# Mixing's state held by pairs of heads: four 64-column state products per batch instead of eight 32-column ones

## The chip, the cores and the metric

The kernel runs on one core of a Trainium2 chip. The metric is device time in microseconds (us) of one execution; lower is better. The time before is 571.9 us, the median of three runs (571.48 to 572.41).

## The reference, cut to what matters

The program is a chunked state-space mixer ("attention" in the names), followed by two MLPs over 3072 tokens with model width 256 and hidden width 2048. For 4 batches, 8 heads, 768 tokens, head width D = 32 and state width N = 16:

```python
for c in range(nc):                        # chunks of tokens
    cum = np.cumsum(log_a, axis=-1)        # log decay inside the chunk
    L = exp(cum[i] - cum[j]) * (i >= j)
    M = (C @ B.T) * L
    y_intra = M @ x                        # inside the chunk
    y_inter = (C @ state) * exp(cum)[:, None]   # from the chunks before
    y = y_intra + y_inter
    state = exp(cum[-1]) * state + (B * exp(cum[-1] - cum)).T @ x
h = softplus(y_all @ w_in) @ w_out         # first MLP
out = (lambda u: u * sigmoid(1.702 * u))(h @ w2_in) @ w2_out
```

Each head has a state of its own, 16 x 32 numbers.

## The kernel before, in words

**Units.** The mixer uses chunks of T = 128 tokens: NC = 6 chunks of NB = 4 batches, 24 sub-blocks s = 4 * chunk + batch, each with 8 heads. The first MLP takes one chunk of all batches (512 tokens) at a time and runs 96 steps t, 16 per chunk, each making one 128-row block of the hidden layer (`g1`) and, two steps later, adding its part of the output (`g2`). While step t works on chunk c, the mixer prepares sub-blocks of chunk c + 1, one sub-block per four steps (k = 0 to 3 is the step inside these four). The second MLP follows after step 95; it uses the `p` products and no mixing.

**Order.** All instructions are issued in the order written (`tc.manual_schedule`), so each engine works its own queue in program order. What the kernel's text does not say, semaphores do: a tile's reader waits for its writer, and a new tile in a pool's slot waits for those who used the slot's tile before. Before step 0 stands a start in which the four sub-blocks of chunk 0 are mixed one after another with the first weights being unpacked beside them (the names `wraw`, `wt`, `w1ih`, `w1il` belong to the unpacking of the 64-bit weights into a high and a low float part).

**Mixing of one sub-block.** `at_load_a` loads the decays: `abz` (for the mask L) and, from chunk 1 on, `ad`, the decays broadcast over 32 partitions per head, by four DMAs on SyncE's queue. `at_scan` makes L on VectorE. `at_small` makes `bs` (B times the decay to the chunk's end) on GpSimd, then the running decay `dc` by two scans on VectorE, and `cd` = C * dc on GpSimd. `at_cb` and `at_m` make M, written over L. `at_y` and `at_u` run for a pair of sub-blocks (s - 1, s with s odd) at k = 2: the state products (`y<-cd,st`), the products with M (`y<-L,px`) and the products that make the state's increment u (`y<-px,bs`). `at_out` copies y into the MLP's input `xh`, `xl`; `at_state` updates the state on VectorE.

**Layout of the state.** A head has a row group of 32 partitions, of which 16 hold the state and the other 16 are zero; heads 0 to 3 lie in the four row groups at g = 0, heads 4 to 7 in the same row groups at g = 1. For odd s the row groups are turned by one (`rows`), so that the eight products of one g of a pair use eight different 32 x 32 pieces of TensorE's array: 16 state products for a pair, each 32 partitions deep, 32 columns of weights wide, 128 columns long.

**PSUM.** Pool `ps_y` has two one-bank tiles, tag y, from the start to the end: sub-blocks use them for y and u, and in the last chunk and in the second MLP the output sums with an odd number (`acc_of`) take them, one bank for each half j of the output. Pool `ps_e` holds six banks until step 0.

**The end of the start.** `at_u(NB - 1)` (the increment of sub-block 3) comes after step 0's `g1`; `at_state(2)` and `at_state(3)` come in steps 1 and 3.

The functions touched by the diff follow with the line numbers of the profile.

Of the kernel before, what the change touches and what calls it, by code (L numbers as in the profile page):

```python
# [34 lines left out]
SX_X, SX_BN, SX_CI, SX_W = 0, 256, 384, 640  # L35
# [8 lines left out]
def mixer_two_mlps(ctx: ExitStack, tc: tile.TileContext, pack_p, pack_q, pack_s, pack_x, a_rows, consts, w1i, w1o, w2i, w2o, out):  # L44
# [20 lines left out]
    cc = at1.tile([P, 2 + P], F32, name="cc")  # L65
    zr = at1.tile([P, T], F32, name="zr")
    mB, mC, eye = cc[:, 0:1], cc[:, 1:2], cc[:, 2:]
# [5 lines left out]
    bs_t = [at1.tile([P, NH, 2, N], F32, name=f"bs{i}") for i in range(2)]  # L73
    state = [at1.tile([P, 2, D], F32, name=f"st{b}") for b in range(NB)]
# [102 lines left out]
    def rows(s, h):  # L177
        r = 32 * ((h + s % 2) % 4)
        return slice(r, r + 32)

# [4 lines left out]
    def at_load_a(s):  # L185
        c, b = divmod(s, NB)
        d = sub.setdefault(s, {})
        d["abz"] = at.tile([P, NH, T], F32, tag="abz", name=f"abz{s}")
        r0 = s * NH
        nc.sync.dma_start(  # L190
            out=d["abz"].rearrange("p h t -> p (h t)"),
            in_=scr_z[r0 : r0 + NH, :].rearrange("(o h) t -> o (h t)", o=1).to_broadcast([P, NH * T]),
        )
        if c > 0:
            d["ad"] = at.tile([P, 2, T], F32, tag="ad", name=f"ad{s}")
            src = scr_a[r0 : r0 + NH, :].rearrange("(g h) t -> h g t", g=2)
            for h in range(4):
                nc.sync.dma_start(out=d["ad"][rows(s, h)], in_=src[h : h + 1].to_broadcast([32, 2, T]))
# [43 lines left out]
    def at_spread(s, half):  # L242
        d = sub.setdefault(s, {})
        if s == 0:
            d["abz", half] = ps_y.tile([P, NH // 2, T], F32, tag="y", name=f"abz{s}_{half}")
# [21 lines left out]
    def at_small(s):  # L267
        c, b = divmod(s, NB)
        d = sub[s]
        if c < NC - 1:  # L270
            (nc.vector if s == 3 else nc.gpsimd).tensor_tensor(
                out=bs_t[s % 2][:, :, 0, :], in0=d["bn"].rearrange("p (h n) -> p h n", h=NH),
                in1=d["L"][:, :, T - 1 : T].to_broadcast([P, NH, N]), op=ALU.mult,
            )
        if c > 0:
            d["dc"] = at.tile([P, 2, T], F32, tag="dc", name=f"dc{s}")
# [4 lines left out]
            d["cd"] = at.tile([P, 2, T], F32, tag="cd", name=f"cd{s}")  # L281
            nc.gpsimd.tensor_tensor(
                out=d["cd"].rearrange("p g t -> p (g t)"), in0=d["dc"].rearrange("p g t -> p (g t)"), in1=d["ci"], op=ALU.mult
            )
# [44 lines left out]
    def y_of(s):  # L329
        if "y" not in sub[s]:  # L330
            sub[s]["y"] = ps_y.tile([P, 512], F32, tag="y", name=f"y{s}")
        return sub[s]["y"]

    def busy(s, n):
        for _ in range(n):
            nc.tensor.matmul(y_of(s)[:, 512 - P :], wz, wz, start=True, stop=True, skip_group_check=True)

    def at_y(*ss):
        for s in ss:
            y_of(s)  # L340


        for g in range(2 if ss[0] >= NB else 0):
            for h in range(4):
                for s in ss:
                    d, r = sub[s], rows(s, h)
                    nc.tensor.matmul(  # L347
                        d["y"][32 * h : 32 * h + 32, g * T : g * T + T], state[s % NB][r, g, :], d["cd"][r, g, :],
                        start=(g == 0), stop=False, skip_group_check=True,
                    )  # L350
        for s in ss:
            d = sub[s]
            for g in range(2):
                for h in range(4):
                    x0 = g * P + h * D
                    nc.tensor.matmul(  # L356
                        d["y"][32 * h : 32 * h + 32, g * T : g * T + T], d["x"][:, x0 : x0 + D], d["M", g][:, h, :],
# [3 lines left out]
    def at_u(s):  # L361
        d = sub[s]
        if s < NSUB - NB:
            for g in range(2):
                for h in range(4):
                    x0 = g * P + h * D
                    nc.tensor.matmul(
                        d["y"][rows(s, h), 256 + g * D : 256 + g * D + D],
                        bs_t[s % 2][:, 4 * g + h].rearrange("p s n -> p (s n)"), d["x"][:, x0 : x0 + D],
                        start=True, stop=True, skip_group_check=True,  # L370
                    )
# [3 lines left out]
    def at_out(s):  # L375
# [6 lines left out]
        y = d["y"][:, 0:256].rearrange("p (g t) -> p g t", g=2)  # L382
# [7 lines left out]
    def at_state(s):  # L390
# [4 lines left out]
        u = d["y"][:, 256 : 256 + 2 * D].rearrange("p (g d) -> p g d", g=2)  # L395
        st = state[b]
        if c == 0:
            if s < 2:
                nc.scalar.activation(st, u, AF.Copy)
            else:  # L400
                nc.vector.tensor_copy(st, u)
            return
        for g in range(2):
# [72 lines left out]
    with tc.manual_schedule():  # L476
# [8 lines left out]
        idle = ps_y.tile([P, 512], F32, tag="y", name="idle")  # L485
# [30 lines left out]
        for i in range(2):  # L516
            nc.gpsimd.memset(bs_t[i][:, :, 1, :], 0.0)
# [90 lines left out]
        w_load(w1i, "1i", 3)  # L608
        early_ctx.close()
# [412 lines left out]
```

## Time and profile before

| what | value |
|---|---|
| median of three runs | 571.9 us |
| the profiled execution | 572.09 us |
| its span in the trace | 570.3 us |
| TensorE busy | 562.7 us, 99% of the span |
| VectorE busy | 452.7 us, 79% |
| ScalarE busy | 338.9 us, 59% |
| GpSimd busy | 122.0 us, 21% |

The profiled execution is 1.8 us longer than its span, which covers the instructions of the engines alone. Busy time is a union: products that run at the same time in different pieces of the array count once. In the trace a float32 product has two records (it passes the array twice); an fp32r product has one. PE stands for TensorE's products, PEld for its weight loads, DVE for VectorE, ACT for ScalarE, POOL for GpSimd and SPq for SyncE's DMA queue.

### The profile page before, as it was taken

Reading aid. Unit: us, or ns where it says so; the run is one execution under the profiler, and the core shown is the slowest. Engines: PE = TensorE matmul, PEld = TensorE weight load, DVE = VectorE, ACT = ScalarE, POOL = GpSimd, SP = SyncE. Lnnn points to the kernel's source line nnn. Section 1 sums busy time; section 2 is a strip of 40 time slices with the busy share of each in tenths; the row PEclk is TensorE's granted clock in tenths of the full one; section 3 lists DMA queues with packets and bytes.
Section 4 is the critical chain, followed back from the end, with each engine's and each line's share of the span. In section 5 each row is a group of like instructions: output and inputs, shape, how many; then the busy total and the mean of one; then the engine's idle time right before and its main releaser. Section 6 shows DMA issues by size and latency. Waiting matters only on the chain.

```text
span 570.3 us, 9042 instructions
## 1 busy us (share of the span) xinstructions
PE 562.7 (99%) x3424; PEld 452.0 (79%) x3424; DVE 452.7 (79%) x683; ACT 338.9 (59%) x571; POOL 122.0 (21%) x105
## 2 busy tenths in 40 slices
PE   9999999999999999999999999999999999999997
PEld 7656687888888888888888788888888888888885
DVE  7997999979787977878898699998976565665654
ACT  4877654534344443435898877866756464664654
POOL 3343474444463544442000000000000000000000
PEclk9999999999999999999999999999999999999999
DMA  8766543343414335410323212000200000100002
GB/s 296 252 227 231 207 167 107 107 150 106 156 62 166 107 111 201 164 62 2 110 77 109 72 38 75 1 1 0 75 0 1 1 0 1 74 1 0 2 0 75
DMA packets 26427, 51.28 MB, mean 90 GB/s; under 512 B 3056, under 2 KB 8848, under 8 KB 26384
## 3 DMA queue, kind: packets, MB, share of 16 engines
q1 hardware_dynamic: 26240, 50.64, 26.1%
q8 instruction: 27, 0.44, 0.3%
q14 instruction: 16, 0.13, 0.1%
q10 hardware_dynamic: 144, 0.07, 0.0%
HBM read 47.35 MB, written 3.34 MB: 89 GB/s over the span
## 4 chain that ended last, share of the span: by engine, by line
PE 84%; DVE 5%; ACT 3%; DMA 3%; issue 1%; SPq 0%; POOL 0%; DVEq 0%; ACTq 0%
PE p L811 19%; PE h L427 19%; PE o L787 8%; PE o L785 8%; PE o L786 8%; PE o L446 6%; PE o L448 6%; PE o L447 6%; PE y L356 2%; DMA wraw_1i<-w1i 2%; PE cb L316 1%; PE y L347 1%; DVE L L262 1%; DVE L L326 1%; DVE gl L85 1%; DMA ad<-scr_a 1%
## 5 line engine op out<-in xcount | busy, mean ns | idle before, releaser
L85 DVE TENSOR_TENSOR gl<-g,gh 128x512 fp32r<-128x512 f32 x180 | 141.8, 789 | 22.7 <-ACT gh L453 21.7
L896 ACT ACTIVATE g<-h 128x512 f32<-128x512 f32 x96 | 57.6, 600 | 107.4 <-PE h L427 97.1
L453 ACT ACTIVATE gh<-g 128x512 fp32r<-128x512 f32 x180 | 113.8, 632 | 5.8
L427 PE MATMUL h<-xh,w1ih 128*128 128x512 f32 x192 | 79.4, 414 | 0.3 <-ACT w1ih L95 0.3
L427 PE MATMUL h<-xl,w1ih 128*128 128x512 f32 x192 | 75.3, 393 | 0.2 <-DVE xl L85 0.2
L817 DVE TENSOR_TENSOR g<-p,x 128x512 f32<-128x512 f32 x72 | 49.6, 689 | 29.6 <-PE p L811 28.1
L446 PE MATMUL o<-gh,w1ol 128*128 128x512 f32 x168 | 66.4, 395 | 0.3 <-DVE w1ol L85 0.3
L447 PE MATMUL o<-gh,w1oh 128*128 128x512 f32 x168 | 65.5, 390 | 0.0
L448 PE MATMUL o<-gl,w1oh 128*128 128x512 f32 x168 | 65.4, 389 | 0.0
L262 DVE TENSOR_TENSOR_SCAN L<-abz,eye 128x1024 f32<-128x1024 f32 (+1 forms) x25 | 64.3, 2580 | 0.8 <-PE abz L252 0.7
L427 PE MATMUL h<-xh,w1il 128*128 128x512 f32 x192 | 59.4, 391 | 0.8 <-DVE w1il L85 0.8
L819 ACT ACTIVATE g<-g 128x512 f32<-128x512 f32 x72 | 45.4, 631 | 20.9 <-DVE g L817 18.5
L88 POOL TENSOR_TENSOR rhs_bd<-tc,pk 64x512 fp32r<-64x512 f32 x32 | 54.9, 1714 | 1.2
L785 PE MATMUL o<-gh,w2ol 128*128 128x512 f32 x120 | 46.8, 390 | 0.4 <-ACT gh L453 0.4
L787 PE MATMUL o<-gl,w2oh 128*128 128x512 f32 x120 | 46.8, 390 | 0.0
L786 PE MATMUL o<-gh,w2oh 128*128 128x512 f32 x120 | 46.7, 389 | 0.0
L819 ACT ACTIVATE g<-p 128x512 f32<-128x512 f32 x24 | 14.3, 596 | 52.4 <-PE p L811 52.3
L427 PEld LDWEIGHTS h<-xh,w1ih 128*128 128x128 f32 x192 | 36.0, 188 | 9.8 <-issue 2.2
L427 PEld LDWEIGHTS h<-xh,w1il 128*128 128x128 f32 x192 | 36.0, 188 | 9.2 <-DVE w1il L85 1.2
L427 PEld LDWEIGHTS h<-xl,w1ih 128*128 128x128 f32 x192 | 36.0, 188 | 9.0 <-issue 2.4
L326 DVE TENSOR_TENSOR L<-cb,L 128x512 f32<-128x512 f32 x40 | 26.9, 682 | 15.9 <-PE cb L316 15.2
L446 PEld LDWEIGHTS o<-gh,w1ol 128*128 128x128 f32 x168 | 31.5, 188 | 7.7 <-DVE w1ol L85 0.7
(183 smaller groups left out, 1058.9 us busy)
## 6 DMA issues: line engine op xcount, KB each, us to landing
abz<-scr_z SPq DMA_DIRECT2D x20, 512.0 KB, 3.8
pk<-pack_s SPq DMA_DIRECT2D x16, 512.0 KB, 4.3
px<-pack_x SPq DMA_DIRECT2D x20, 320.0 KB, 3.0
wraw_1i<-w1i SPq DMA_DIRECT2D x8, 512.0 KB, 4.9
wraw_1o<-w1o SPq DMA_DIRECT2D x8, 512.0 KB, 4.5
wraw_2i<-w2i SPq DMA_DIRECT2D x8, 512.0 KB, 3.5
wraw_2o<-w2o SPq DMA_DIRECT2D x8, 512.0 KB, 3.3
out<-ot SPq DMA_DIRECT2D x11, 256.0 KB, 2.0
```

Source lines behind the costliest of these rows:

```text
L85: nc.vector.tensor_sub(o, x, y)
L262: nc.vector.tensor_tensor_scan(out=d["L"][:, h].rearrange("p h t -> p (h t)"), data0=ab.rearrange("p h t -> p (h t)"), data1=eye8[:, h].re ...
L427: nc.tensor.matmul(h, w[:, k, f], x[:, k, :], start=(n == 0), stop=(n == 5))
L446: nc.tensor.matmul(a, w1ol[:, m, o], d["gh"], start=first, stop=False)
L447: nc.tensor.matmul(a, w1oh[:, m, o], d["gh"], start=False, stop=False)
L448: nc.tensor.matmul(a, w1oh[:, m, o], d["gl"], start=False, stop=last)
L453: nc.scalar.activation(d["gh"], d["g"], AF.Copy)
L785: nc.tensor.matmul(a, wl, d["gh"], start=first, stop=False)
L786: nc.tensor.matmul(a, wh, d["gh"], start=False, stop=False)
L787: nc.tensor.matmul(a, wh, d["gl"], start=False, stop=last)
L811: nc.tensor.matmul(dst, w, x, start=start and i == 0, stop=i == 2, skip_group_check=not start)
L819: nc.scalar.activation(d["g"], src, AF.Gelu_apprx_sigmoid)
```

## The change

Two neighbouring heads share a row group of 32 partitions, 16 for each, so that the eight heads of a sub-block fill the 128 partitions once. The state tile is [128, 64]: for each head's 16 rows it holds the 32 columns of both heads of the pair, and a mask (`own`, 1 in the head's own columns) gives `state_own`, a masked copy made on GpSimd by `at_state`. A state product is then 32 partitions deep and 64 columns of weights wide, four for a sub-block. The increments u are made by pairs as well: four products with 64 columns. `bs` has no zero half any more; `ad` is one DMA of [128, 128]; `dc` is one scan, `cd` is 128 columns wide, the state update is one instruction. Both sub-blocks of a pair share one tile of two banks in `ps_y` (bank g for heads 4g to 4g + 3). In the start the tiles of y come from `ps_a`, which is released with `ps_e`; so `at_u(3)`, `at_state(2)` and `at_state(3)` are moved ahead of step 0. The odd output sums take `ps_y`'s two banks as one tile.

```diff
-SX_X, SX_BN, SX_CI, SX_W = 0, 256, 384, 640
+SX_X, SX_BN, SX_CI, SX_W = 0, 256, 384, 512
...
-    ps_y = ps_ctx.enter_context(tc.tile_pool(name="ps_y", bufs=2, space=PSUM))
-
     early_ctx = ExitStack()
+    ps_a = early_ctx.enter_context(tc.tile_pool(name="ps_a", bufs=2, space=PSUM))
     ps_e = early_ctx.enter_context(tc.tile_pool(name="ps_e", bufs=1, space=PSUM))
...
-    cc = at1.tile([P, 2 + P], F32, name="cc")
+    cc = at1.tile([P, 2 + P + 2 * D], F32, name="cc")
...
-    bs_t = [at1.tile([P, NH, 2, N], F32, name=f"bs{i}") for i in range(2)]
-    state = [at1.tile([P, 2, D], F32, name=f"st{b}") for b in range(NB)]
+    bs_t = [at1.tile([P, NH, N], F32, name=f"bs{i}") for i in range(2)]
+    state = [at1.tile([P, 2 * D], F32, name=f"st{b}") for b in range(NB)]
+    state_own = [at1.tile([P, 2 * D], F32, name=f"so{b}") for b in range(NB)]
...
-            d["ad"] = at.tile([P, 2, T], F32, tag="ad", name=f"ad{s}")
-            src = scr_a[r0 : r0 + NH, :].rearrange("(g h) t -> h g t", g=2)
-            for h in range(4):
-                nc.sync.dma_start(out=d["ad"][rows(s, h)], in_=src[h : h + 1].to_broadcast([32, 2, T]))
+            d["ad"] = at.tile([P, T], F32, tag="ad", name=f"ad{s}")
+            nc.sync.dma_start(out=d["ad"], in_=scr_a[r0 : r0 + NH, :].unsqueeze(1).to_broadcast([NH, N, T]))
...
-            for g in range(2):
-                nc.vector.tensor_tensor_scan(
-                    out=d["dc"][:, g, :], data0=d["ad"][:, g, :], data1=zr, initial=1.0, op0=ALU.mult, op1=ALU.add
-                )
...
+            nc.vector.tensor_tensor_scan(out=d["dc"], data0=d["ad"], data1=zr, initial=1.0, op0=ALU.mult, op1=ALU.add)
+            d["cd"] = at.tile([P, T], F32, tag="cd", name=f"cd{s}")
+            nc.gpsimd.tensor_tensor(out=d["cd"], in0=d["dc"], in1=d["ci"], op=ALU.mult)
...
     def y_of(s):
...
+            if s < NB:
+                y = ps_a.tile([P, 512], F32, tag="y", name=f"y{s}")
+                d["y"], d["u"] = y[:, 0 : 2 * T].rearrange("p (k t) -> p k t", k=2), y[:, 2 * T : 2 * T + 2 * D]
+                d["spare"] = y[:, 512 - P :]
+            else:
+                y = ps_y.tile([P, 2, 512], F32, tag="y", name=f"y{s}")
+                for i in range(2):
+                    sub[s + i]["y"] = y[:, :, T * i : T * i + T]
+                    sub[s + i]["u"] = y[:, 0, 2 * T + 2 * D * i : 2 * T + 2 * D * i + 2 * D]
...
-        for g in range(2 if ss[0] >= NB else 0):
-            for h in range(4):
-                for s in ss:
-                    d, r = sub[s], rows(s, h)
-                    nc.tensor.matmul(
-                        d["y"][32 * h : 32 * h + 32, g * T : g * T + T], state[s % NB][r, g, :], d["cd"][r, g, :],
-                        start=(g == 0), stop=False, skip_group_check=True,
-                    )
+        for p in range(4 if ss[0] >= NB else 0):
+            r = slice(32 * p, 32 * p + 32)
+            for s in ss:
+                nc.tensor.matmul(
+                    sub[s]["y"][64 * (p % 2) : 64 * (p % 2) + 64, p // 2], state_own[s % NB][r], sub[s]["cd"][r],
+                    start=(s == ss[0]), stop=False, skip_group_check=True,
+                )
...
     def at_u(s):
...
+            for p in range(4):
+                nc.tensor.matmul(
+                    d["u"][32 * p : 32 * p + 32], bs_t[s % 2][:, 2 * p : 2 * p + 2].rearrange("p h n -> p (h n)"),
+                    d["x"][:, 2 * D * p : 2 * D * p + 2 * D], start=True, stop=True, skip_group_check=True,
+                )
...
     def at_state(s):
...
+        if s < 2:
+            nc.scalar.activation(st, u, AF.Copy)
+        elif c == 0:
+            nc.vector.tensor_copy(st, u)
+        else:
             nc.vector.scalar_tensor_tensor(
-                out=st[:, g, :], in0=st[:, g, :], scalar=d["dc"][:, g, T - 1 : T], in1=u[:, g, :], op0=ALU.mult, op1=ALU.add
+                out=st, in0=st, scalar=d["dc"][:, T - 1 : T], in1=u, op0=ALU.mult, op1=ALU.add
             )
+        nc.gpsimd.tensor_tensor(out=state_own[b], in0=st, in1=own, op=ALU.mult)
...
             if c >= NC - 1 and c % 2:
-                acc[c] = [ps_y.tile([P, TB], F32, tag="y", name=f"o{t}_{j}") for j in range(2)]
+                o = ps_y.tile([P, 2, TB], F32, tag="y", name=f"o{t}")
+                acc[c] = [o[:, j] for j in range(2)]
...
-        for i in range(2):
-            nc.gpsimd.memset(bs_t[i][:, :, 1, :], 0.0)
...
         w_load(w1i, "1i", 3)
+        at_u(NB - 1)
+        at_state(2)
+        at_state(3)
         early_ctx.close()
+        ps_y = ps_ctx.enter_context(tc.tile_pool(name="ps_y", bufs=1, space=PSUM, reuse_waits="tile"))
...
             g1(t, *W1, xh[c], xl[c])
-            if t == 0:
-                at_u(NB - 1)
...
-            if t in (1, 3):
-                at_state(2 + t // 2)
```

## Rows read from the trace of the kernel before

**Rows 1.** The page's first part: busy us, share of the span, instructions.

```profile
PE 562.7 (99%) x3424; PEld 452.0 (79%) x3424; DVE 452.7 (79%) x683; ACT 338.9 (59%) x571; POOL 122.0 (21%) x105
```

**Rows 2.** Timeline of PE, 41 to 52 us: start us, us, instructions merged.

```profile
42.44 0.67 PE L347 MATMUL y<-cd,st 32*32 32x128 f32 x32
43.04 1.09 PE L356 MATMUL y<-L,px 128*32 128x128 f32 x32
43.94 0.48 PE L367 MATMUL y<-px,bs 128*32 128x32 f32 x32
44.35 0.50 PE L427 MATMUL h<-xh,w1ih 128*128 128x512 f32 x1
```

**Rows 3.** Timeline of PE up to 42.50 and 42.64, then up to 43.97 and 43.995 us.

```profile
42.44 0.34 PE L347 MATMUL y<-cd,st 32*32 32x128 f32 x8
...
42.44 0.45 PE L347 MATMUL y<-cd,st 32*32 32x128 f32 x16
...
43.94 0.21 PE L367 MATMUL y<-px,bs 128*32 128x32 f32 x4
...
43.94 0.24 PE L367 MATMUL y<-px,bs 128*32 128x32 f32 x8
```

**Rows 4.** Timeline of PE in the start: products of `at_cb_early` for two sub-blocks.

```profile
17.14 0.73 PE L295 MATMUL cb<-x 32*128 32x256 f32 x8
17.67 0.62 PE L295 MATMUL cb<-pq 32*128 32x256 f32 x8
```

**Rows 5.** Groups by form, PEld: busy us, mean ns of one, idle before.

```profile
L347 PEld LDWEIGHTS y<-cd,st 32*32 32x32 f32 x320 | 4.0, 104 | 4.0 <-issue 4.0
...
L336 PEld LDWEIGHTS y<-wz 128*128 128x128 f32 x22 | 2.7, 191 | 0.7 <-issue 0.7
```

**Rows 6.** Groups by form, DVE and POOL, of the instructions that the change resizes.

```profile
L278 DVE TENSOR_TENSOR_SCAN dc<-ad,zr 128x128 f32<-128x128 f32 x40 | 15.9, 437 | 0.0
...
L282 POOL TENSOR_TENSOR cd<-dc,px 128x256 f32<-128x256 f32 x20 | 15.7, 786 | 34.5 <-DVE dc L278 22.5 <-PE h L427 8.5 <-issue 3.5
...
L404 DVE SCALAR_TENSOR_TENSOR st<-st,dc,y 128x32 f32<-128x32 f32 x32 | 5.5, 230 | 0.0
...
L271 POOL TENSOR_TENSOR bs<-x,L 128x128 f32<-128x128 f32 x3 | 1.4, 480 | 9.4 <-DVE L L262 6.5 <-PE cb L295 2.9
```

**Rows 7.** Tile `ad`, its DMA issues: ns min/median/max, first and last start.

```profile
L198 SPq DMA_DIRECT2D ad<-scr_a x80: 303/420/1334, 9.0 to 241.1; - x80
```

**Rows 8.** Timeline of the start, 14 to 34 us; in brackets idle before and releaser.

```profile
14.27 0.21 ACT L399 ACTIVATE st<-y 128x64 f32<-128x64 f32 x1
...
14.44 0.62 POOL L271 TENSOR_TENSOR bs<-x,L 128x128 f32<-128x128 f32 x1 [2.90 <-PE cb L295]
...
15.09 1.29 DVE L326 TENSOR_TENSOR L<-cb,L 128x512 f32<-128x512 f32 x2 [0.30 <-POOL bs L271]
...
21.39 0.73 PE L427 MATMUL h<-xh,w1ih 128*128 128x512 f32 x2
...
21.99 0.74 DVE L85 TENSOR_TENSOR xl<-y,xh 128x256 fp32r<-128x256 f32 x2
...
31.86 0.50 PE L427 MATMUL h<-xh,w1ih 128*128 128x512 f32 x1 [0.31 <-ACT w1ih L95]
...
33.86 0.73 PE L427 MATMUL h<-xh,w1il 128*128 128x512 f32 x2 [0.80 <-DVE w1il L85]
```

**Rows 9.** Waits over the whole span: us in total, times, longest us.

```profile
ACT xh L387 <- PE y L367: 5.5, 7, 2.4
```

**Rows 10.** Timelines around 67 and 91 us: two later waits of TensorE for VectorE.

```profile
67.98 0.50 PE L446 MATMUL o<-gh,w1ol 128*128 128x512 f32 x1 [0.27 <-DVE w1ol L85]
...
91.71 0.30 PEld L316 LDWEIGHTS cb<-rhs_bd,lb 128*128 128x128 f32 x2 [0.53 <-DVE L L326]
```

**Rows 11.** Timeline around 328 us: the odd sum changes from 5 to 7.

```profile
328.16 0.68 DVE L471 COPY x<-o 128x512 f32<-128x512 f32 x1
328.28 0.39 PE L785 MATMUL o<-gh,w2ol 128*128 128x512 f32 x1
```

More of the change, by code (lines that the diff above doesn't have):

```diff
@@ L64, in mixer_two_mlps @@
     eye8 = at1.tile([P, NH, T], F32, name="eye8")
-    cc = at1.tile([P, 2 + P], F32, name="cc")
+    cc = at1.tile([P, 2 + P + 2 * D], F32, name="cc")
     zr = at1.tile([P, T], F32, name="zr")
-    mB, mC, eye = cc[:, 0:1], cc[:, 1:2], cc[:, 2:]
+    mB, mC, eye, own = cc[:, 0:1], cc[:, 1:2], cc[:, 2 : 2 + P], cc[:, 2 + P :]
     scr_z = dram.tile([NSUB * NH, T], F32, name="scr_z")
@@ L244, in at_spread @@
         if s == 0:
-            d["abz", half] = ps_y.tile([P, NH // 2, T], F32, tag="y", name=f"abz{s}_{half}")
+            d["abz", half] = ps_a.tile([P, NH // 2, T], F32, tag="y", name=f"abz{s}_{half}")
         elif half == 0:
@@ L271, in at_small @@
             (nc.vector if s == 3 else nc.gpsimd).tensor_tensor(
-                out=bs_t[s % 2][:, :, 0, :], in0=d["bn"].rearrange("p (h n) -> p h n", h=NH),
+                out=bs_t[s % 2], in0=d["bn"].rearrange("p (h n) -> p h n", h=NH),
                 in1=d["L"][:, :, T - 1 : T].to_broadcast([P, NH, N]), op=ALU.mult,
@@ L275, in at_small @@
         if c > 0:
[L276 to L284 removed]
+            d["dc"] = at.tile([P, T], F32, tag="dc", name=f"dc{s}")
+            nc.vector.tensor_tensor_scan(out=d["dc"], data0=d["ad"], data1=zr, initial=1.0, op0=ALU.mult, op1=ALU.add)
+            d["cd"] = at.tile([P, T], F32, tag="cd", name=f"cd{s}")
+            nc.gpsimd.tensor_tensor(out=d["cd"], in0=d["dc"], in1=d["ci"], op=ALU.mult)
     def at_cb_early(s, tags=None, host=None, groups=(0, 1)):
@@ L329, in y_of @@
     def y_of(s):
-        if "y" not in sub[s]:
-            sub[s]["y"] = ps_y.tile([P, 512], F32, tag="y", name=f"y{s}")
-        return sub[s]["y"]
+        d = sub[s]
+        if "y" not in d:
+            if s < NB:
[7 more added lines that the diff above has]
+                    sub[s + i]["u"] = y[:, 0, 2 * T + 2 * D * i : 2 * T + 2 * D * i + 2 * D]
+        return d["y"]
     def busy(s, n):
+        y_of(s)
         for _ in range(n):
-            nc.tensor.matmul(y_of(s)[:, 512 - P :], wz, wz, start=True, stop=True, skip_group_check=True)
+            nc.tensor.matmul(sub[s]["spare"], wz, wz, start=True, stop=True, skip_group_check=True)
     def at_y(*ss):
@@ L363, in at_u @@
         if s < NSUB - NB:
[L364 to L371, printed above, removed]
+            for p in range(4):
[3 more added lines that the diff above has]
+                )
     xh, xl = {}, {}
@@ L381, in at_out @@
         o = slice(b * T, b * T + T)
-        y = d["y"][:, 0:256].rearrange("p (g t) -> p g t", g=2)
+        y = d["y"]
         if s < 2:
@@ L394, in at_state @@
             return
-        u = d["y"][:, 256 : 256 + 2 * D].rearrange("p (g d) -> p g d", g=2)
+        u = d["u"]
         st = state[b]
[L397 to L403, printed above, removed]
+        if s < 2:
[3 more added lines that the diff above has]
+        else:
             nc.vector.scalar_tensor_tensor(
-                out=st[:, g, :], in0=st[:, g, :], scalar=d["dc"][:, g, T - 1 : T], in1=u[:, g, :], op0=ALU.mult, op1=ALU.add
+                out=st, in0=st, scalar=d["dc"][:, T - 1 : T], in1=u, op0=ALU.mult, op1=ALU.add
             )
+        nc.gpsimd.tensor_tensor(out=state_own[b], in0=st, in1=own, op=ALU.mult)
     def at_pe(s, k):
@@ L483, in mixer_two_mlps @@
         at_load_q(0)
-        idle = ps_y.tile([P, 512], F32, tag="y", name="idle")
+        idle = ps_a.tile([P, 512], F32, tag="y", name="idle")
         wz = hid.tile([P, TB], F32, tag="gh", name="wz")[:, 0:P]
@@ L973, in _lay_out @@
     bn = Bc.transpose(0, 1, 3, 2, 4).reshape(NSUB, T, NH * N)
-    ci = Cc.reshape(NC, NB, 2, 4, T, N).transpose(0, 1, 3, 5, 2, 4)
-    ci = np.broadcast_to(ci[:, :, :, None], (NC, NB, 4, 2, N, 2, T)).copy()
-    ci[:, 1::2] = np.roll(ci[:, 1::2], 1, axis=2)
-    ci = ci.reshape(NSUB, P, 2 * T)
+    ci = Cc.swapaxes(3, 4).reshape(NSUB, P, T)
     def pairs(v):
@@ L1001, in _consts @@
     mc = ((p // 32) % 2 == 1)[:, None]
-    return np.concatenate([mb, mc, np.eye(P)], axis=1).astype(np.float32)
+    return np.concatenate([mb, mc, np.eye(P), np.where(mb == np.repeat([0, 1], D), 1, 0)], axis=1).astype(np.float32)
 def kernel(x, a, B, C, moe_w_in, moe_w_out, moe2_w_in, moe2_w_out):
```

6 lines of the change are left out of this document (1 added, 5 removed).

## The prediction

> **What bounds the kernel now.** I read the busy shares first, then TensorE's timeline round one pair of sub-blocks, the groups by form for each edited instruction, and last the list of waits and the start. TensorE is busy 562.7 of 570.3 us [rows 1]: the reader is to see that no other engine's work counts unless TensorE waits for it. So the change is worth what it takes from TensorE's own stream, plus what it does to the few waits there are. One pair's mixing in that stream has three stretches: state products from 42.44 to 43.04 (0.60 us), products with M to 43.94 (0.90), increments to 44.35 (0.41) [rows 2]. There are ten pairs, eight of them with increments. All of what the change could save there is thus 10 x 0.60 + 8 x 0.41 = 9.3 us at the very most.
>
> **State products: half as many, equally long.** The 32 records of a pair do not run one after another. Eight have started by 42.50, sixteen by 42.64 [rows 3]: rounds of eight, 0.11 us apart (the timeline's ends, 42.78 and 42.89, say the same), because the eight products of one g lie in eight different 32 x 32 pieces of the array. Each piece takes two products of two records each, four rounds, and four times 0.11 plus the change of tile shape makes the 0.60. After the change a pair has eight products; sub-blocks s - 1 and s share row group and columns, so only four different pieces (32 x 64) are in use, and each again takes two products of two records. Four rounds again: the number of products halves and the parallelism halves with it. What is added is the wider first weight load: 104 ns at 32 columns, 191 at 128 [rows 5], so (an estimate on the line between them) 133 at 64, about 0.03 us more once per pair, later loads running under the round before. Ten pairs: **+0.3 us**. Bounds: if the time went with the number of products, 0.30 less per pair, -3.0 us; if a product waiting for its piece held up those behind it, +0.66 per pair, +6.6 (the rival below).
>
> That the four pieces do run at once although the written order is (piece 0, piece 0, piece 1, piece 1, ...) needs products to pass one another. They do: in the start the written order is two products of `x`, two of `pq` in the same row groups, two of `x` and two of `pq` in the other row groups, and the trace has all eight records of `x` before the first of `pq` [rows 4]. The Trainium skill, "TensorE: Matmul & The Clock Gate", section "Part 3: Packing small matmuls", says the contrary: products start and end in strict program order and only weight loads are pulled ahead. By it the eight products would need five steps of 0.22 us instead of two, and the sum would be 6.6 us higher; rows 4 speak against it, and the measurement decides.
>
> **Increments.** Rounds of four records, 0.03 us apart [rows 3], eight rounds for a pair, 0.25 us, and 0.16 of lead and drain make the 0.41. After it there are four rounds of 64 columns; at 0.11 for 128 columns a round is 0.055, together 0.22. Saved 0.03 per pair, **-0.25 us** for eight. Bounds: nothing, and half of 0.41 for eight, -1.6.
>
> **Products with M** keep number, shape and order: nothing.
>
> **VectorE, GpSimd, SyncE.** Per sub-block VectorE loses a scan of 0.44 us (20 in all) and, 16 times, one of two updates of 0.23; the remaining update has 64 columns, a little longer. GpSimd's `cd` of 0.79 is halved in width, about 0.4 saved, and the masked copy is added; from `bs` at 0.48 (128 columns) and `cd` at 0.79 (256) I estimate 0.3 for 64 columns [rows 6]. SyncE issues 20 `ad` transfers for 80, each 0.42 [rows 7]. None of it is on TensorE's stream, so in the loop it is worth nothing except where TensorE waits. In the loop the copy stands before the next `bs` on GpSimd, whose product with M follows over a microsecond later on VectorE (an estimate: a low part, a scan and an update stand between).
>
> Two waits in the loop do fall to it. At 67.98 TensorE waited 0.27 for a weight's low part on VectorE, at 91.71 a weight load waited 0.53 for M on VectorE [rows 10], of which I count half, since a load can wait under the product before it. Ahead of each stand scans of `dc` of 0.44 that go. I take both waits as gone: **-0.4 us** (0.27 and some 0.1 for the slow first product after a stop) and **-0.3 us**. Bound: nothing. With VectorE no longer late, the products' own order is next.
>
> **The start.** Here VectorE, not TensorE, sets the pace up to 33.86, where TensorE waits 0.80 for `w1il`, after 0.31 at 31.86 for `w1ih` [rows 8]. Three things touch it. First, the masked copy for sub-block 0 stands on GpSimd ahead of `bs` of sub-block 2 and has to wait for ScalarE's copy of the state, which ends at 14.48; the copy's 0.3 and a hand-over put `bs` near 15.0 instead of 14.44, though with less beside it than its 0.62 (a free one takes 0.48 on the mean [rows 6]), and VectorE's products with M at 15.09 were already waiting for `bs` [rows 8]: 0.4 us late. Secondly, two state copies of some 0.2 each come ahead of VectorE's scan of sub-block 4, one scan of `dc` (0.4) goes behind it; the copies disappear later: about even by 33.86. Thirdly, `at_u(3)` comes ahead of step 0. It writes the bank that `xl` of sub-block 3 still reads, and the trace shows that PSUM's users of one bank wait for each other even in other columns (`xh` waits for the increments, 7 times [rows 9]). So step 0, which began at 21.39, waits for the `xl` that ends at 22.73, then for 0.3 of increments, and begins near 23.1; since its own last two products waited for `xl` anyhow, what is left is about 0.9 us at step 1. Behind it stand steps 1 to 3, and these run into the waits of 31.86 and 33.86, 1.1 us by the rows, which swallow it: cost nothing, and up to 0.5 if VectorE is early there. In sum **+0.4 us**; bounds -0.4 (VectorE's lighter load wins) and +1.1 (nothing of the copies is recovered).
>
> **Odd sums.** They now take one two-bank tile. Sum 7 starts at 328.28 in the bank that ScalarE had emptied, while VectorE copies the other half of sum 5 from 328.16 to 328.84 [rows 11]. As one tile, sum 7 must wait for both: 0.56 and some 0.1 of slow first product, **+0.65 us**. At the two later changes of odd sums the copies end first. Bound: nothing, if halves of a tile are tracked separately.
>
> **The sum**, against the profiled execution's 572.09: +0.3 - 0.25 - 0.4 - 0.3 + 0.4 + 0.65 = +0.4, so 572.5; that execution lies 0.2 above the median of the runs, so I say 572.3 for the median. Against 571.9 a difference below 0.2% (1.1 us) is about what a measurement of this kernel cannot tell from no change: this is a forecast of no change.
>
> **Rivals.**
> Held order (slower, other side): the second product for a busy piece holds up the products of other pieces. Place: the state stretch; price: the first piece's second product can start only after 0.22, and then each piece's first runs beside the piece before's second, five steps for two, 0.66 per pair, 572.3 + 6.3 = 578.6. It decides as soon as a pair's state stretch is longer than 0.72 us (1.1 us over ten pairs). Rows 4 speak against; chance 0.08.
> Longer start (slower): GpSimd's copies for sub-blocks 1 to 3 stand ahead of the scaling of weights, and and the 0.9 us at step 1 is not wholly swallowed: +1.1 in place of +0.4, and the waits at 67.98 and 91.71 stay: 572.3 + 1.4 = 573.7. For it: VectorE and GpSimd are both in the start's chain. Against: a scaled weight is joined only after ScalarE has unpacked its other part. Chance 0.13.
> Half the products, half the time (faster): the change does in time what it does in number: 572.3 - 3.3 = 569.0. Against: the rounds of eight. Chance 0.08.
> Lighter engines (faster): no wait at 328.28, a start 0.4 shorter, increments at half of 0.41: 572.3 - 0.65 - 0.8 - 1.35 = 569.5, and up to 570.8 with only part of it; chance 0.12. For it speaks VectorE's share in every wait of the rows, against it that the start gains copies.
> The forecast itself says that the change does not do in time what its words say; chance 0.59.
>
> **How the numbers follow.** Predicted 572.3, its own range 570.8 to 573.0 by the 0.2% bound. Faster 0.08 + 0.12 = 0.20, same 0.59, slower 0.08 + 0.13 = 0.21. The range takes in most of the lighter engines and of the longer start, and leaves out held order and half time, 0.16 together: 570.2 to 573.7.
>
> **What would show it.** Right: a pair's state stretch stays at 0.60 to 0.65 with 16 records of 32 x 64 in rounds of four, 0.11 apart; increments fall to near 0.38; step 0 starts near 23; no wait at 67.98 or 91.71; a wait of TensorE for VectorE's copy near 328.3. Wrong: a state stretch near 0.3 or near 1.25; step 4 starting more than 1 us later than 31.86; sum 7 starting beside the copy.

## The result: 1.3% slower, and the profile after

The changed kernel takes 579.34 us (median of six runs, 578.41 to 581.29), the kernel before beside it 572.15 (571.48 to 573.04): a ratio of 1.0131, 95% interval 1.0112 to 1.0149. The forecast was 572.3 in a range up to 573.7, so it was wrong by 7 us and on the side to which I had given 0.21. The profiled execution took 579.38 us, its span 577.6 for 570.3 before.

The busy part of the page says already what kind of loss it is: TensorE is busy 0.6 us longer than in [rows 1], in a span that is 7.3 longer. It waits. VectorE's 10 us of relief bought nothing.

```profile
PE 563.3 (98%) x3104; PEld 451.9 (78%) x3104; DVE 442.2 (77%) x647; ACT 339.9 (59%) x571; POOL 128.3 (22%) x123
```

The list of TensorE's waits names them (us in total, times, longest):

```profile
PE o L780 <- ACT ot L462: 4.0, 3, 2.0
PE h L419 <- ACT w1ih L95: 1.5, 1, 1.5
PE o L439 <- ACT x L462: 1.1, 1, 1.1
...
PE y L361 <- DVE xl L85: 0.9, 1, 0.9
...
PE h L419 <- DVE w1il L85: 0.7, 1, 0.7
PE o L780 <- DVE x L464: 0.6, 1, 0.6
```

L462 and L464 are the copies of a finished sum out of PSUM (`finish`), `ot` and `x` their targets, L780 and L439 the products of the sums: 5.7 us of waits at the odd sums, where I had written one of 0.56. In the kernel before, the same list has no wait for such a copy; the one wait there at a product of the second MLP's sums is for an operand:

```profile
PE o L785 <- ACT gh L453: 0.4, 1, 0.4
```

**The pair** does what the prediction said, nearly to the digit. Timeline of the pair that answers to [rows 2], then the state products cut off at 45.80 and 45.90 us, as in [rows 3]:

```profile
45.68 0.69 PE L343 MATMUL y<-cd,so 32*64 32x128 f32 x16
46.29 1.08 PE L352 MATMUL y<-L,px 128*32 128x128 f32 x32
47.19 0.41 PE L361 MATMUL y<-px,bs 128*32 128x64 f32 x16
47.53 0.50 PE L419 MATMUL h<-xh,w1ih 128*128 128x512 f32 x1
...
45.68 0.36 PE L343 MATMUL y<-cd,so 32*64 32x128 f32 x4
...
45.68 0.47 PE L343 MATMUL y<-cd,so 32*64 32x128 f32 x8
```

The starts give 0.61 us for the state (0.60 before), 0.90 for M (0.90), 0.34 for the increments (0.41). Half the records come in rounds of four, 0.11 apart, where there were rounds of eight.

**Where the time went** is read by taking the same product in both traces. The product behind the wait of 31.86 us [rows 8] starts at 33.65, 1.8 late. The one behind the first pair starts at 47.53 instead of 44.35 [rows 2], 3.2 late. The last products of half 0 of sum 5 start 1.7 late, the kernel before first, the changed kernel second:

```profile
320.73 0.39 PE L446 MATMUL o<-gh,w1ol 128*128 128x512 f32 x1
```

```profile
322.46 0.39 PE L439 MATMUL o<-gh,w1ol 128*128 128x512 f32 x1
```

The first stop at an odd sum follows (1.06, at 326.40). Sum 7 starts at 330.71 instead of 328.28 [rows 11], 2.4 late, of which 0.57 is its own wait. The end is 7.3 late. So: 3.2 lost by the end of the first pair, 1.5 of it won back up to sum 5, and 5.6 lost from there on, where the listed waits are 5.7.

**The start.** GpSimd, VectorE and TensorE, with the idle time before an instruction and what ended it in brackets:

```profile
26.34 2.71 POOL L398 TENSOR_TENSOR so<-st,cc 128x64 f32<-128x64 f32 x2 [4.81 <-DVE st L393]
29.02 1.51 POOL L126 TENSOR_SCALAR wt_1i<-wraw_1i 128x512 f32<-128x512 f32 x1
30.50 0.41 POOL L265 TENSOR_TENSOR bs<-px,L 128x128 f32<-128x128 f32 x1
...
26.31 2.28 DVE L256 TENSOR_TENSOR_SCAN L<-abz,eye 128x1024 f32<-128x1024 f32 x1
...
30.95 0.93 DVE L315 TENSOR_TENSOR L<-cb_0k,L 128x512 f32<-128x512 f32 x1 [1.99 <-POOL bs L265]
...
22.93 0.73 PE L419 MATMUL h<-xh,w1ih 128*128 128x512 f32 x2
...
30.25 1.88 PE L437 MATMUL o<-g,x 128*128 128x512 f32 x4
33.65 0.50 PE L419 MATMUL h<-xh,w1ih 128*128 128x512 f32 x1 [1.52 <-ACT w1ih L95]
...
35.51 1.22 PE L419 MATMUL h<-xh,w1il 128*128 128x512 f32 x2 [0.67 <-DVE w1il L85]
36.53 3.02 PE L437 MATMUL o<-g,x 128*128 128x512 f32 x4
```

Read it from the bottom. TensorE waits 1.52 for a weight half, VectorE before that 1.99 for `bs`, and GpSimd makes `bs` only at 30.50, because a scaling of 1.51 stands before it, and before that the masked copies of sub-blocks 2 and 3, which first wait 4.81 for VectorE's state copies and then take 2.71. Of this the first copy takes 2.34, the longest of all twenty (min, median and max in ns):

```profile
L398 POOL TENSOR_TENSOR so<-st,cc x20: 297/746/2337, 14.6 to 226.4; 128x64 f32<-128x64 f32 x20
```

Then four products that took 1.88 at 30.25 take 3.02: the granted clock fell (below, e5).

**The odd sums.** ScalarE's copy and TensorE's product at sum 7:

```profile
410.59 0.58 ACT L462 ACTIVATE ot<-o 128x512 f32<-128x512 f32 x1
...
411.22 0.50 PE L780 MATMUL o<-gh,w1ol 128*128 128x512 f32 x1 [2.05 <-ACT ot L462]
```

Half 0 of the sum is finished first, and ScalarE copies it once its `g` and `gh` are done. TensorE goes on to the last products of half 1 and stands for 2.05 us until that copy ends. The same stop occurs at sums 5, 9 and 11 (1.06, 1.24, 0.69).

### The profile page after: what moved, and what is told of

The parts are those of the page before. It is cut to its first block, busy times and chain, and to the rows that moved or that the text cites. A ratio compares the mean times of both kernels' runs of the same rounds, so it can differ in the third digit from the quotient of the medians.

```text
span 577.6 us, 8314 instructions
## 1 busy us (share of the span) xinstructions
PE 563.3 (98%) x3104; PEld 451.9 (78%) x3104; DVE 442.2 (77%) x647; ACT 339.9 (59%) x571; POOL 128.3 (22%) x123
## 4 chain that ended last, share of the span: by engine, by line
PE 89%; ACT 3%; DVE 3%; issue 1%; POOL 0%; DVEq 0%; POOLq 0%
PE h L419 22%; PE p L806 18%; PE o L780 7%; PE o L781 7%; PE o L782 7%; PE o L439 7%; PE o L440 6%; PE o L441 6%; PE o L437 3%; PE y L352 2%; PE cb L305 1%; PE y L343 1%; ACT gh L446 0%; ACT g L814 0%; DVE L L256 0%
## 5 line engine op out<-in xcount | busy, mean ns | idle before, releaser
L439 PE MATMUL o<-gh,w1ol 128*128 128x512 f32 x168 | 66.4, 395 | 1.1 <-ACT x L462 1.1
L256 DVE TENSOR_TENSOR_SCAN L<-abz,eye 128x1024 f32<-128x1024 f32 (+1 forms) x25 | 61.5, 2467 | 0.8 <-PE abz L246 0.7
L780 PE MATMUL o<-gh,w2ol 128*128 128x512 f32 x120 | 46.8, 390 | 0.6 <-DVE x L464 0.6
L439 PEld LDWEIGHTS o<-gh,w1ol 128*128 128x128 f32 x168 | 31.5, 188 | 8.8 <-ACT x L462 1.5
```

The lines of the kernel that those rows point to most:

```text
L256: nc.vector.tensor_tensor_scan(out=d["L"][:, h].rearrange("p h t -> p (h t)"), data0=ab.rearrange("p h t -> p (h t)"), data1=eye8[:, h].re ...
L439: nc.tensor.matmul(a, w1ol[:, m, o], d["gh"], start=first, stop=False)
L780: nc.tensor.matmul(a, wl, d["gh"], start=first, stop=False)
```

## The experiments

Each ratio is against the kernel before, run on the same chip; `after` stands for 1.0131.

| kernel | us | ratio, 95% interval |
|---|---|---|
| e1 both copies of an odd sum late | 577.00 | 1.0070 (1.0058 to 1.0083) |
| e2 start's masked copies late | 578.65 | 1.0095 (1.0080 to 1.0109) |
| e3 both | 574.73 | 1.0038 (1.0023 to 1.0053) |
| e4 before, increments of sub-block 3 first | 573.33 | 1.0006 (0.9997 to 1.0015) |
| e5 products in the wait | 580.33 | 1.0131 (1.0115 to 1.0148) |
| e6 odd sums in two tiles | 573.85 | 1.0019 (1.0009 to 1.0028) |
| e7 e6 and e2 | 571.92 | 0.9982 (0.9974 to 0.9991) |
| e8 e7, increments of sub-block 3 back | 571.08 | 0.9969 (0.9957 to 0.9980) |
| e9 e6, only copies 2 and 3 late | 571.91 | 0.9982 (0.9973 to 0.9991) |
| e10 e7 with half the state products | 569.22 | 0.9935 (0.9921 to 0.9949) |
| e11 e6, scan ahead of state copies | 574.29 | 1.0032 (1.0021 to 1.0044) |
| e12 e6, copies 2 and 3 behind the scaling | 572.19 | 0.9994 (0.9984 to 1.0003) |

**e1: is it the copy of half 0 that half 1 waits for?**

```diff
-                if last:
+                if last and c % 2 == 0:
                     finish(c, j)
+                elif last and j == 1:
+                    finish(c, 0)
+                    finish(c, 1)
```

> The changed kernel, but for the odd sums of the second MLP: the copy of half 0 is issued only when the products of half 1 have been issued too, so no copy can hold up a write to the other half of the two-bank tile. Theory A (a two-bank tile makes the last products of half 1 wait for ScalarE's copy of half 0; shifts of 2.3, 1.5 and 0.9 us at 406.6, 488.2 and 565.7): the waits at L780 for ScalarE's copy go, the time falls by 4.5 to 4.8 us from 579.3, to 574.5 to 575.0, and the run's shift against the kernel before no longer grows behind 330 us. Theory B (the time behind 330 us is lost to the turn of the sums, the next sum waiting for the copies of the last but one): no change, 578.8 to 579.8; as both copies are later, it may even be slower.

It fell by 0.61%, 3.5 us, less than expected. The waits for ScalarE's copy of half 0 are gone, but later copies make the next sum wait longer for its turn:

```profile
PE o L780 <- DVE x L464: 1.5, 1, 1.5
...
PE o L780 <- DVE ot L464: 0.6, 1, 0.6
```

So a part of the waits changed its place. Theory A names the cause, and its price was too high for this cure.

**e6: one tile of two banks, or two tiles?** Products and copies are those of the change, and each half keeps a bank of its own; what differs is what counts as one tile. (So that `ps_y` can be closed ahead of sum 5, the other pools of PSUM are laid out from its other end; the lines below do not show this.)

```diff
-                o = ps_y.tile([P, 2, TB], F32, tag="y", name=f"o{t}")
-                acc[c] = [o[:, j] for j in range(2)]
+                if not ps_p:
+                    y_ctx.close()
+                    ps_p.append(ps_ctx.enter_context(tc.tile_pool(name="ps_p", bufs=1, space=PSUM, ...)))
+                acc[c] = [ps_p[0].tile([P, TB], F32, tag=f"p{j}", ...) for j in range(2)]
```

> The changed kernel, with each odd sum of the second MLP in two tiles of one bank instead of one tile of two banks; banks and products are the same. Theory A (the waits for a copy of the other half come from the two halves being one tile): besides the 4.5 to 4.8 us of the three late waits, the wait at 328.3 (0.8 us) goes: 5.3 to 5.6 us less than 579.3, that is 573.7 to 574.0, and no product of an odd sum waits for a copy of its other half. Theory B (the copies are late for the next use of the same bank, whatever the tile): no change, 578.8 to 579.8.

573.85, as theory A has it; by the ratios it is 1.12%, 6.4 us, more than its 5.3 to 5.6, since the kernel before took 572.92 on this chip. And no product of an odd sum waits for a copy any more. TensorE's longest waits now:

```profile
PE h L419 <- ACT w1ih L95: 1.5, 1, 1.5
...
PE y L361 <- DVE xl L85: 0.9, 1, 0.9
PE o L441 <- DVE w1ol L85: 0.8, 1, 0.8
PE h L419 <- DVE w1il L85: 0.7, 1, 0.7
```

The last products of half 0 of sum 5 start at 322.25 here, 1.5 later than in the kernel before, and the span is 1.7 longer: of the 5.6 lost from there on, 0.2 is left, so it was the tile's. The wait for `w1ol` is that of [rows 10]: with TensorE less late it is back.

**e2 and e3: the masked copies of the start.**

```diff
-        nc.gpsimd.tensor_tensor(out=state_own[b], in0=st, in1=own, op=ALU.mult)
+        if c > 0:
+            at_mask(b)          # the same copy, as a function of b
 ...
+            if t == 1:
+                for b in range(NB):
+                    at_mask(b)
```

> The changed kernel, but the four masked copies of the start are issued on GpSimd behind step 1 instead of ahead of the scaling of weights and of bs. Theory A (those copies, two of them beside VectorE's scan in 2.7 us, hold up bs and with it VectorE and ScalarE, and TensorE then waits 1.5 and 0.7 us at steps 3 and 4 and loses its clock there): 2.5 to 3.2 us less than 579.3, that is 576.1 to 576.8; the granted clock of 35 to 40 us is back at 1.00 (0.66 with the copies). Theory B (the increments and state copies moved ahead of step 0 make the start late): no change, 578.8 to 579.8, and the clock between 35 and 40 us stays low.

> The changed kernel with both edits: copies of odd sums issued together, and the start's masked copies behind step 1. Theory A (two separate causes that add up): 7.0 to 8.0 us less than 579.3, that is 571.3 to 572.3. Theory B (they overlap, or one only hides the other): less than the sum of the two single runs by over 1 us.

e2 fell by 0.36%, 2.1 us, a bit less than expected (its 578.65 lies above the 576.8 of theory A); e3 by 0.32% against e1, so the two edits add up to within 0.04%. Theory A of both holds for the waits; e3's 574.73 lies above its 571.3 to 572.3, since e1 gives less than was expected of it. In e2's profile the granted clock is 1.00 from 30 to 40 us, and yet its runs lie between 577.13 and 579.14. The windows (busy us, granted clock, DMA share, GB/s) show where the clock of the profiled execution, the one of 579.14, fell instead: from 24 to 28 us, and again behind the stop of 2.05 at sum 7.

```profile
24.00:28.00 4.00, 4.00 (x12) 0.57 0.55 145
...
411.00:412.00 1.00, 1.00 (x4) 0.50 0.38 143
```

e3, which is the same kernel as e2 up to sum 5, has in the first of these windows:

```profile
24.00:28.00 4.00, 4.00 (x18) 1.00 0.53 140
```

Behind the same wait of 1.3 us for `xl`, the granted clock fell near 1.2 GHz in one execution and stayed at 2.4 in the other.

**e5: is the clock a loss of its own?** Eight products of 128 columns that nobody reads, ahead of the step whose wait is 1.52:

```diff
+            if t == 4:
+                warm = ps_c.tile([P, 4 * T], F32, tag="cb", name="warm")
+                for _ in range(8):
+                    nc.tensor.matmul(warm[:, 0:T], wz, wz, start=True, stop=True)
             g1(t, *W1, xh[c], xl[c])
```

> The changed kernel with eight products of 128 columns, whose result nobody reads, put on TensorE ahead of step 4, in the time in which it waits for VectorE's weight part. Theory A (of the start's loss some 1.2 to 1.4 us is the granted clock, which falls after the two waits): the granted clock between 35 and 40 us rises from 0.66 to 0.9 or more and the time falls by 1.0 to 1.4 us, to 577.9 to 578.3. Theory B (the products of 35 to 40 us are slow for another reason, such as operands that arrive late): no change or up to 0.9 us more, the time of the eight products.

The products stand in the wait, from 32.19 to 33.89 us, and the wait for `w1ih` is gone from the list. No change in time: 1.0131 again. The window of 35 to 40 us of the changed kernel, the same of e6 (same waits, no such products), and two of e5:

```profile
35.00:40.00 5.00, 4.49 (x9) 0.66 0.84 252
```

```profile
35.00:40.00 5.00, 4.49 (x14) 1.00 0.92 279
```

```profile
35.00:40.00 5.00, 4.32 (x15) 1.00 0.79 270
412.00:416.00 4.00, 4.00 (x12) 0.57 0.35 131
```

My expectation is not borne out. The fall in the changed kernel's profile was one execution's: e6 has the same waits there and a clock of 1.00. In e5 it fell at 412 us instead, behind the stop of sum 7.

What a fall costs depends on what comes behind it. At 35 to 40 us it was swallowed: the product of 44.35 in the kernel before starts at 47.53 in the changed kernel and at 46.17 in e6, 1.4 apart, and by 322 us (322.46 and 322.25) 0.2 of that is left, mostly since the wait of 0.8 for `w1ol` that e6 has in between is missing in the changed kernel. At 412 us it stayed: from the product at 389.34 to that at 413.60, 24.25 in the kernel before and in e6, the changed kernel takes 26.59 with the stop of sum 7 and the clock at 1.00, e5 and e2 take 28.21 with the same stop and the fall. So the stop costs 2.3 and the fall behind it 1.6, in those executions that have it. Three of the six runs of the changed kernel have a mean granted clock of 1.000 (578.4 to 579.3 us), three of 0.997 (579.4 to 581.3); where the two that were not profiled lost it, no run settles.

**e9: which of the four copies?** On e6; copies 0 and 1 stay in their place.

```diff
-        nc.gpsimd.tensor_tensor(out=state_own[b], in0=st, in1=own, op=ALU.mult)
+        if c > 0 or b < 2:
+            at_mask(b)          # 2 and 3 behind step 1, as in e2
```

> The changed kernel with odd sums in two one-bank tiles, and of the start's masked copies only those of sub-blocks 2 and 3 behind step 1; those of sub-blocks 0 and 1 stay where the change has them. Theory A (the two copies beside VectorE's scan, 2.71 us together, are what holds up the start): as with all four late, 571.6 to 572.3. Theory B (the copy of sub-block 0 ahead of bs of sub-block 2 is as much to blame, since VectorE waits for that bs): half of the 1.9 us between all in place (573.85) and all late (571.9) stays, 572.6 to 573.2.

Theory A: 571.91, as with all four late (571.92). The 0.4 that I had put on the copy of sub-block 0 does not show, within intervals of some 0.5 us.

**e11: what makes a copy of 64 columns take 2.34 us?** On e6, VectorE scans first and copies the states then.

```diff
         at_u(NB - 1)
+        at_scan(NB)
         at_state(2)
         at_state(3)
 ...
-        at_scan(NB)
```

> The changed kernel with odd sums in two one-bank tiles, all masked copies in their place, and on VectorE the scan of sub-block 4 ahead of the state copies of sub-blocks 2 and 3, so that their masked copies come behind that scan. Theory A (the masked copy of 2.34 us is held by the scan beside it): no masked copy is longer than 0.85 us; but as the scaling of 1.51 and bs still stand behind them on GpSimd, bs ends no earlier than 30.3 and the time stays at 573.3 to 574.3. Theory B (the copy is slow for another reason, as that it reads what VectorE has just written): one copy still takes over 2 us.

Theory A, in both parts. The long scan no longer stands beside the two copies, only that of `dc`, 0.41 from 28.92; they take 0.73 together, 0.47 the first, although they still read what VectorE has just written. And as scaling and `bs` still stand behind them the time is 574.29, no better than e6:

```profile
28.95 0.73 POOL L398 TENSOR_TENSOR so<-st,cc 128x64 f32<-128x64 f32 x2 [6.98 <-DVE st L393]
29.65 1.51 POOL L126 TENSOR_SCALAR wt_1i<-wraw_1i 128x512 f32<-128x512 f32 x1
31.13 0.41 POOL L265 TENSOR_TENSOR bs<-px,L 128x128 f32<-128x128 f32 x1
```

**e12: the copy, or what is queued behind it?** On e6, the two copies one place later on GpSimd, behind the scaling.

```diff
         wt = w_scale(*W1_units[0], nc.gpsimd)
+        at_mask(2)
+        at_mask(3)
```

> The changed kernel with odd sums in two one-bank tiles, and the masked copies of sub-blocks 2 and 3 on GpSimd behind the scaling of the weight that follows them in the change, still ahead of bs and still beside VectorE's scan. Theory A (what costs is that the scaling, which could run 5 us earlier, is queued behind copies that wait for VectorE, and bs behind it): the first of the two copies still takes over 2 us, bs ends near 29.5 instead of 30.9, and 1.2 to 1.8 of the 1.9 us between 573.85 and 571.9 come back, 572.1 to 572.6. Theory B (the slow copy itself is the cost, wherever it stands ahead of bs): no gain, 573.4 to 574.3.

572.19, 0.25% or 1.4 us below e6: theory A. The copies are as slow as ever (2.71 together, the longest 2.34), but the scaling is done in the time in which GpSimd waited, and `bs` ends 1.2 earlier:

```profile
21.73 1.53 POOL L126 TENSOR_SCALAR wt_1i<-wraw_1i 128x512 f32<-128x512 f32 x1
26.59 2.71 POOL L402 TENSOR_TENSOR so<-st,cc 128x64 f32<-128x64 f32 x2 [3.33 <-DVE st L393]
29.26 0.41 POOL L265 TENSOR_TENSOR bs<-px,L 128x128 f32<-128x128 f32 x1
```

**e4: increments of sub-block 3 ahead of step 0, alone.** Built on the kernel before.

```diff
         w_load(w1i, "1i", 3)
+        at_u(NB - 1)
+        at_state(2)
+        at_state(3)
         early_ctx.close()
```

> The kernel before, with the increments of sub-block 3 and the two state copies of sub-blocks 2 and 3 moved ahead of step 0, as the change moves them. Theory A (the move is swallowed by the waits of the start): within 0.5 us of 571.9 to 572.2; step 0 begins near 23 instead of 21.4, and step 4 at its old time. Theory B (the move makes the start late): 573.5 to 575, with a low granted clock between 35 and 40 us.

1.0006, an interval that holds 1 and reaches to 0.9 us: theory A by the time, the move is swallowed. Step 4 is not at its old time in the profiled execution: it starts at 33.64 for 31.86, since there the clock fell behind the wait for `xl` (0.57 from 24 to 28 us). That costs nothing here: the five runs with a mean granted clock of 0.996 or 0.997 take 572.7 to 573.4 us, the other six 572.5 to 573.7.

**e7: both costs removed.** The edits of e6 and e2.

> The changed kernel with odd sums in two tiles of one bank, and the start's masked copies behind step 1. Theory A (both causes removed, and what is left is the gain of the pairs, some 0.5 us, and of the two waits at 68 and 92 us, some 0.85, less a start that is 0.4 to 0.6 longer): 570.8 to 571.6, against 571.9 to 572.2 of the kernel before. Theory B (the pairs by 32-row groups are themselves no gain on the time, and something else of the change is lost elsewhere): 572.5 or more.

571.92, ratio 0.9982: faster than the kernel before by 1.0 us. Theory A, if 0.3 above its bounds, on a chip on which the kernel before took 572.71. Of the waits of [rows 10], the one for `w1ol` is still there (0.25 at 67.77). The weight load that waited 0.53 for M at 91.71 still waits, 0.22 at 91.14, but under the product before: the product behind it starts 0.22 after that one, where it started 0.50 after it.

**e8: the late step 0 put back as well.** e7, with the increments and state copies where the kernel before has them, and the masked copies behind steps 1 and 3. (`ps_a` then stays open up to step 3, and `ps_y` is opened there; the lines below do not show this.)

```diff
-        at_u(NB - 1)
-        at_state(2)
-        at_state(3)
         early_ctx.close()
 ...
             g1(t, *W1, xh[c], xl[c])
+            if t == 0:
+                at_u(NB - 1)
 ...
+            if t in (1, 3):
+                at_state(2 + t // 2)
```

> The kernel with odd sums in two one-bank tiles and late masked copies, and with the increments of sub-block 3 behind step 0 and the state copies of sub-blocks 2 and 3 behind steps 1 and 3 again, as in the kernel before; the masked copies stand behind steps 1 and 3. Theory A (the late step 0 is swallowed by VectorE's pace in the start, and costs only the granted clock that in some executions falls behind its wait of 1.3 us): step 0 begins near 21.5, the time is 0 to 1 us below the 571.9 of the same kernel without this edit, and the runs with a mean granted clock of 0.997 become rare. Theory B (the late step 0 costs its 1.5 us in every execution): 570.2 to 570.6. Theory C (the state copies moved back lengthen VectorE's chain behind step 1): 572.3 or more.

571.08, ratio 0.9969: the fastest here, 1.8 us below the kernel before. Step 0 begins at 21.82. All six runs have a mean granted clock of 0.999 or more, of e7's twelve runs four. That is theory A; the intervals of e7 and e8 overlap, so the 0.8 us between them are not settled. In its profiled execution, at 572.29 the slowest of the six, TensorE has a wait of 0.73 for `xl` at 74.93 that no other kernel lists; no run tells why.

**e10: what does the number of state products cost?** e7 without the four state products of a pair's odd sub-block, whose part of y is then left out.

```diff
-            for s in ss:
+            for s in ss[:1]:
                 nc.tensor.matmul(
                     sub[s]["y"][64 * (p % 2) : ...
```

> The kernel with odd sums in two one-bank tiles and late masked copies, without the four state products of the odd sub-block of each pair (its state part is left out of the result): each of the four pieces of the array has one product of two records instead of two of two. Theory A (rounds: the time goes with the number of records that one piece takes one after another): two rounds of 0.11 fewer, the state stretch falls from 0.616 to about 0.40, ten pairs, 2.2 us less than the 571.9 of the same kernel with all products, 569.7. Theory B (the time goes with the number of products): the stretch halves to 0.31, 3.1 us less, 568.8. Theory C (the change of tile shape is what costs): no change.

The state stretch is 0.38, from 117.32 to 117.70:

```profile
117.32 0.45 PE L343 MATMUL y<-cd,so 32*64 32x128 f32 x8
117.70 1.08 PE L352 MATMUL y<-L,px 128*32 128x128 f32 x32
```

That is two rounds fewer, as theory A has it (0.40), not half of 0.61; ten pairs give 2.3 us, and 2.7 were measured. In these kernels the count of products decides only where it changes how many records one piece of the array takes in turn.

## Why the prediction was wrong

**State products: right.** Four rounds before and after, 0.61 against 0.60, with e10 as the test. The rival "half the time" falls with it. So does "held order", which was to be told by a stretch over 0.72 us: its 578.6 comes near the measured 579.3, and for a wrong reason. A total that fits a rival says nothing until the place that the rival names has been looked at. The strict order of products that the Trainium skill gives ("TensorE: Matmul & The Clock Gate", "Part 3: Packing small matmuls") disagrees with the trace here: by it the stretch would be near 1.25, an estimate from the rounds of 0.11.

**Increments: right in kind, too small.** 0.07 a pair, 0.56 for eight, where I had 0.25.

**The waits of [rows 10]: half right.** The wait for M no longer stops TensorE, 0.28 by the rows (e7), where I had 0.3. The wait for `w1ol` is missing in the changed kernel, where TensorE is 3.2 late; with TensorE in time it is 0.25 again in e7, and not listed in e8. So VectorE's lighter load alone did not remove it.

**The late step 0: right.** It begins at 22.93 (I had 23.1) and is swallowed (e4).

**Odd sums: this step failed.** "As one tile, sum 7 must wait for both" was right, and measured 0.57. But I looked only at the change from one sum to the next, and wrote "At the two later changes of odd sums the copies end first". The two halves of a sum are not finished together: the copy of half 0 falls between its last product and the last products of half 1, and in one tile these wait for it, at every odd sum. I had counted the readers of the old tile and not the reader of the other half. Listed waits of 5.7 us in the place of 0.65; 6.4 us by e6. The 0.7 between may be the clock that in some executions falls behind such a stop; that is not settled.

**The start: this step failed too.** I costed the masked copy of sub-block 0, which does not show in the time (e9), and left those of 2 and 3 to the rival "longer start", which named the place, ahead of the scaling, and added 0.7 for the whole start, with a copy at 0.3. They cost 2.1 us (e6 to e7). They wait 4.81 for VectorE with work queued behind them that could have run; this is 1.4 of the 2.1 (e12). And the first takes 2.34 for its 0.3, from 26.34 to 28.68, beside a scan from 26.31 to 28.59; that the scan is the reason is shown (e11), what it costs by itself is not: the other 0.7 lies within the intervals of e12 and e7, and e11 removes the long copy but starts both later and wins nothing. The 0.3 was low beyond this, the median of the twenty copies being 0.75. The trace of the kernel before had rows of this kind in it: GpSimd's products of another form, beside VectorE's scans. First the group (min, median and max ns), then GpSimd and VectorE round 72 us, then the second of the two products alone:

```profile
L88 POOL TENSOR_TENSOR rhs_bd<-tc,pk x32: 1287/1675/3157, 72.2 to 258.4; 64x512 fp32r<-64x512 f32 x32
...
72.23 4.52 POOL L88 TENSOR_TENSOR rhs_bd<-tc,pk 64x512 fp32r<-64x512 f32 x2
...
72.54 3.13 DVE L262 TENSOR_TENSOR_SCAN L<-abz,eye 128x1024 f32<-128x1024 f32 x1
...
73.60 3.16 POOL L88 TENSOR_TENSOR rhs_bd<-tc,pk 64x512 fp32r<-64x512 f32 x1
```

Two of these products take 4.52 for twice 1.68, the second, issued during the scan, 3.16 of it; and the scan, issued during the first, takes 3.13 where the free one takes 2.28. The Trainium skill states the rule ("SBUF — State Buffer", "Who interferes with whom" and "Summary: rules for kernel authors"): a VectorE instruction with two inputs in SBUF and a GpSimd instruction that reads SBUF exclude each other, and the later one stands until the earlier has ended. The trace agrees: the copy issued 0.03 behind the scan ends 0.09 behind it. It does not agree for one scaling on GpSimd, which reads one tile of SBUF: in the kernel before, from 47.78 to 49.30, it took 1.52 as ever, and the scan issued at 48.44 its 2.28. An estimate by a mean over instructions that ran free was the wrong row for one that runs beside a scan.

**The account.** From the changed kernel to e7 the ratio falls by 0.0149, 0.0112 by the tiles and 0.0037 by the masked copies. The two steps that failed make the error: 6.4 for 0.65 and 2.1 for 0.4 are 7.5 us too little, and the forecast was 7 too low. What is left of the change is a gain of 1.0 us (0.5 to 1.5 by the interval), where the other terms of my sum, the state products, the increments and the two waits, come to 0.65.

## What to carry to other kernels

When two buffers become one, list for each half who reads it and who writes the other half at that time, through the whole life of the buffer and not only where it is handed on; the cure here was to keep the storage and split the tile. An instruction added to an in-order queue is costed by what it waits for and what is queued behind it, and its duration is taken from rows with the same neighbour on the other engine. Halving the number of small products saved nothing here, where each piece of the array takes as many records in turn as before.

## What the runs showed of the hardware that was not expected

A GpSimd copy of 128x64 beside a VectorE scan of operands in SBUF: 2.34 us, and 0.73 for two of them where the long scan is done and only one of 0.41 stands beside them (e11). The granted clock, 2.4 GHz nearly throughout, fell to about half for some three or four us behind a wait of 0.7 to 2 us in some executions (0.57 at 24 to 28 us in e2, 0.66 at 35 to 40 in the changed kernel, 0.57 at 412 to 416 in e5), and in others behind the same wait it did not (e3, e6, and the changed kernel at 412 to 416). The fall at 35 us was swallowed by later waits, those at 410 to 416, with no such wait behind them, cost 1.6 us: what such a stop costs in all can't be read from one profile.
